# First two rows of a fused delta-rule and two-MoE kernel: an explicit numbered order, beta by row loads, paired norms, low halves on VectorE

## The chip, the cores and the metric

The kernel runs on one core of a Trainium2 chip. The metric is the device time of one execution in microseconds. A core has TensorE (PE; its weight loads are PEld), VectorE (DVE), ScalarE (ACT), GpSimd (POOL) and SyncE (SP, which issues most DMAs). Each engine works through its own queue in the order in which the program was written; semaphores hold an instruction until what it reads is there.

## The reference

Three layers follow each other: a delta-rule recurrence over 768 tokens for 4 x 8 heads of width 48, then two feed-forward layers on the 3072 tokens of width 384.

```python
k_n = k / (np.linalg.norm(k, axis=-1, keepdims=True) + 1e-06)
for t in range(S):                       # state: (B, H, D, D)
    kt, vt, bt = (k_n[:, :, t], v[:, :, t], beta[:, :, t, None])
    y[:, :, t] = np.einsum('bhd,bhde->bhe', q[:, :, t], state)
    v_old = np.einsum('bhde,bhd->bhe', state, kt)
    state = state + bt[:, :, :, None] * np.einsum('bhd,bhe->bhde', kt, vt - v_old)
...
xn = x / np.sqrt(np.mean(x * x, axis=-1, keepdims=True) + 1e-06) * rms_g
x = (silu(xn @ w_gate) * (xn @ w_val)) @ w_out
...
h = x @ w_in
out = (h * np.tanh(softplus(h))) @ w_out2
```

## The kernel before, in words

The recurrence is computed in 12 rows (chunks) of 64 tokens; two rows make a segment. A row needs the inverse of a triangular matrix made of beta and the Gram matrix of its normalised keys. The steps of a row are the stages of `chain_row` (L795): turn q (`q0`, `q1`), residual `r`, state product `y`, masked scores `p`, `v` (values, with ScalarE's copies at L863), state update `k` (L907, L912), outputs `o0`, `o1`, and the hand-over to the feed-forward layer `s`, `x`. Some stages work four rows ahead: norms `nA` (`norm`, L422), scaling `nB` (`scale_k`, L448), turning `c0`, `c1` (`turn_k`, L460) and the Gram product `g` (`products`, L471).

The inverse for segments 1 to 5 is made by `inlane` (L518), a long series of VectorE instructions (L514 to L610) that starts with one of ScalarE (L513) and is finished by `merge32` (L618) on TensorE and ScalarE. For segment 0 there is a quicker way for one row at a time: `quick_lane` (L647), some 29 VectorE instructions from L658 to L729, and then `quick_products` (L735), a chain of small products and copies between TensorE, VectorE (L750) and ScalarE (L758, L769, L630, L640). Row 2 needs what `inlane(1)` gives, row 4 what `inlane(2)` gives, and so on; `lanes` (L780) runs them side by side with the rows.

The feed-forward weights come as raw 64-bit floats and are converted to a high and a low fp32r half: `prepare_half` (L123) has ScalarE's Abs (L139), four VectorE operations on tile t (L144, L147, L152, L155), ScalarE's high copy (L166) and GpSimd's low subtraction (L169). `convs` (L173) runs twelve such halves for the pairs of part A, the part of the first layer that `gated` (L219) works on beside the rows. Part A's units are handed out per row by `DUE`: 0, 6, 5, then 11. After the last row what is left of part A and all of the rest are TensorE work with little waiting.

The order of the queues is written by Python generators. `merge` (L38) draws the next step from the stream that is least far in relation to its planned total; each row's loop merges the row with part A, conversion, `lanes` and some warm-up products (`warm`, L1019). The first row's start is a sequence of its own: norms one at a time, k0 scaled by VectorE and the others by GpSimd, T and G for rows 0 and 1, `quick_lane(0)` with 26 warm-up products, then a merge of `quick_products(0)` with the norms of k2 and k3 and `quick_lane(1)`; `inlane(1)` starts within row 0. beta reaches its layouts `bq` and `bl` by 32 small DMAs in `setup` (L357): eight issued by ScalarE and eight by SyncE (L363), sixteen by SyncE (L418).

Of the kernel before, what the change touches and what calls it, by code (L numbers as in the profile page):

```python
# [8 lines left out]
F32 = mybir.dt.float32  # L9
F32R = mybir.dt.float32r  # L10
# [10 lines left out]
    XB=2, WE=16, RB=4, TB=3, LANE=15.7, XL=1, HH=0, DPRE=5, WU0=24, WU1=35, WARM=[0, 0], CVS=[2.6, 9.0, 5.0, 13.1, 0], CVA=12, CVT=12.22, CVB0=0, CVB1=1.238, CVC=2.31, PSD=1, INV=1, Q=[0, 2.7, 1.2, 9.9, 0, 18.8, 2.8, 3.0, 11.5, 3.0, 11.0, 19.4], W=[22, 26], SQ=6, CVP=0, NE=2, BQ=3, NU=6, CVN=1, CVE=14.671, CVD=4.076, OFF=6.0,  # L21
    ROW="r nA q0 q1 S p T nB y X v Y k c0 o0 c1 o1 g".split(),
    R0="r q0 q1 p nA v k o0 o1 s0 nB s1 x0 c0 c1 g".split(),
    R2="r nA Y q0 q1 p nB y v k c0 o0 c1 o1 g".split(),
    R1="r nA q0 Y q1 y p nB v k o0 o1 s0 s1 x0 c0 c1 g".split(),
    DUE=[0, 6, 5, 11],
    PRE="t10 t11 c g1 c c w1 | t20 t21 g2 t30 t31 g3".split(),
    C=dict(n=0.2, q=0.5, r=1.4, y=1.1, p=1.2, v=1.2, o=0.9, k=1.2, s=0.1, x=0.45, c=0.4, d=0.4, g=1.2, h=1.2),
)

# [38 lines left out]
def kernel(  # L69
# [48 lines left out]
    count = [0]  # L118

    def prepare(get_pool, key, cut, act=True, **kw):  # L120
        return [prepare_half(half, get_pool, key, cut, act, kw) for half in range(2)]

    def prepare_half(half, get_pool, key, cut, act, kw):  # L123
# [19 lines left out]
        count[0] += 1  # L143
        (nc.gpsimd if count[0] <= P["CVP"] else nc.vector).tensor_scalar(  # L144
# [24 lines left out]
        nc.gpsimd.tensor_tensor(out=lo, in0=tv, in1=hi.bitcast(F32), op=ALU.subtract)  # L169
# [3 lines left out]
    def convs(pairs, wait=0):  # L173
# [5 lines left out]
        yield from delay(wait)  # L179
# [101 lines left out]
    def phase_b1():  # L281
# [33 lines left out]
        even, odd, top = (qc[:, 96 + i:97 + i] for i in range(3))  # L315
        NK = 5
# [9 lines left out]
        kT_t, A_t, X11_t, v_t, x_t, nr_t = {}, {}, {}, {}, {}, {}  # L326
# [30 lines left out]
        def setup():  # L357
            qsrc = beta[:, :, 0:2 * C].rearrange("b (j e) (r f h t) -> e f r (b j) h t", e=2, r=2, f=2, t=16)
            def load_bq(r, queue=nc.sync):
                for g in range(4):  # L360
                    for bp in range(2):
                        o = g * 32 + bp * 16
                        queue.dma_start(  # L363
                            out=bq[o:o + 16, r], in_=qsrc[(g // 2) ^ bp, g % 2, r, bp * 8:bp * 8 + 8]
                        )

            load_bq(0, nc.scalar)
            for r in range(4):
                load_k(r)
                nc.vector.memset(khp[r][:, :, D:64], 0.0)  # L370
                if r == 1:
                    load_q(0)
            load_bq(1)
# [16 lines left out]
            nc.vector.memset(X_[:, 0:272].rearrange("p (i x) -> p i x", x=17)[:, :, 0:1], 1.0)  # L390
            nc.vector.tensor_reduce(
# [20 lines left out]
            bsrc = beta.rearrange("b (j e) (s r f t) -> e f r (b j) s t", e=2, r=2, f=2, t=32)  # L412
            for e in range(2):
                for f in range(2):
                    for r in range(2):
                        for bp in range(2):
                            p0 = (e ^ bp) * 64 + f * 32 + r * 16 + bp * 8
                            nc.sync.dma_start(out=bl[p0:p0 + 8], in_=bsrc[e, f, r, bp * 8:bp * 8 + 8])  # L418
            load_k(4)
            nc.sync.dma_start(out=gT, in_=rms_g.rearrange("(k p) -> p k", p=128))  # L420

        def norm(r, sq=None):  # L422
# [6 lines left out]
            ss = ch.tile([128, 16], F32, tag="ss", name="ss", bufs=2)  # L429
            nc.vector.tensor_reduce(out=ss, in_=sq, axis=AX.X, op=ALU.add)  # L430
            nr = ch.tile([128, 16], F32, tag="nr", name="nr", bufs=2)
            if r < P["SQ"]:
                rt = ch.tile([128, 16], F32, tag="rn", name="rt", bufs=2)
# [14 lines left out]
        def scale_k(r, eng=nc.gpsimd):  # L448
            if r >= NR:
                return  # L450
            nr, kr = nr_t.pop(r), khp[r % NK][:, :, 0:D]
            rn = ch.tile([128, 16], F32, tag="rn", name="rn", bufs=2)
# [552 lines left out]
        for m in range(FA):  # L1005
            gens.append(prepare(lambda: wa, ("g", m), cols(w_gate, m)))
            gens.append(prepare(lambda: wa, ("v", m), cols(w_val, m)))
        for m in range(FA):
            gens.append(prepare(lambda: wa, ("o", m), rows(w_out1, m)))
        cv = convs(gens)  # L1010
# [17 lines left out]
        W_ = P["W"]  # L1028
        Q = P["Q"]
        sq = [xp.tile([128, KD, T], F32R, tag="xh", name="sq", bufs=XB) for _ in range(2)]  # L1030
        sq = [flat(t)[:, 0:16 * D].rearrange("p (u d) -> p u d", d=D) for t in sq]
        run(warm(W_[0]), norm(0), scale_k(0, nc.vector), norm(1, spare), scale_k(1))
        chain0 = chain_row(0)

        def ahead_of(names):
            for x in names:
                if x[0] == "t":
                    r, i = int(x[1]), int(x[2])
                    yield from turn_k(r, i, pre(i) if r else None)
                elif x[0] == "g":  # L1040
                    r = int(x[1])
                    yield from products(r)
                elif x[0] == "n":
                    yield from norm(int(x[1]), sq[int(x[1]) - 2])
                elif x[0] == "s":
                    yield from scale_k(int(x[1]))
                elif x[0] == "w":
                    yield from warm(W_[int(x[1])])
                elif x[0] == "c":
                    next(chain0)  # L1050
                    yield 1.0

        PRE = []
        for x in P["PRE"]:
            if x == "|" or not PRE:
                PRE.append([])
            if x != "|":
                PRE[-1].append(x)
        run(turn_k(0, 0), turn_k(0, 1), products(0))
        merge((quick_lane(0), 12), (ahead_of(PRE[0]), 6.0))  # L1060

        def reset():
# [4 lines left out]
        first = quick_products(0)  # L1067
        next(first)
        merge(
            (first, 5.0),  # L1070
            (seq(*[f(r, *a) for r in (2, 3) for f, a in ((norm, (sq[r - 2],)), (scale_k, ()))], quick_lane(1)), 12.5),
            (seq(delay(14.0), ahead_of(PRE[1])), 20.0),
            (budget(cv, Q[6]), Q[7]),
        )
        lane, laned, left = lanes(merges(1)), [0.0], []
        M1A = 4.0 * FA + KD
        ps_ds = [ps_d]
        part_a = gated((ps_u, ps_ds, hp, tp), range(FA), range(NR), get_xa, finish_a, next_x)
        for sg in range(NSEG):
            for rl in range(2):  # L1080
                r = 2 * sg + rl
                streams = [(chain_row(r) if r else chain0, cost(r))]
                due = P["DUE"][r] if r < len(P["DUE"]) else P["DUE"][-1]
                if due > 0:
                    off = P["OFF"] if r == 1 else 1.5 if r == 2 else 0
# [3 lines left out]
                if r < len(P["WARM"]):  # L1089
                    streams.append((warm(P["WARM"][r]), 0.22 * P["WARM"][r] + 0.1))  # L1090
                if r == 0:
                    lane1 = seq(reset(), inlane(1))
# [202 lines left out]
```

## Time and profile before

| | us |
|---|---|
| median of 3 runs | 1223.62 (1223.1 to 1226.09) |
| the profiled execution's own time | 1223.5 |
| its span, first to last instruction | 1221.8 |
| TensorE busy | 1125.6 (92%) |
| VectorE busy | 721.7 (59%) |
| ScalarE busy | 561.8 (46%) |
| GpSimd busy | 438.6 (36%) |

Times in the timeline count from the start of the span. The granted clock is the share of TensorE's full clock: 1.0 is 2.4 GHz, 0.5 is 1.2 GHz, and a stretch in between is a mean over both. A busy share over the whole span mixes stages with different limits, so the stages are looked at one by one. In a timeline row the last bracket gives idle time before the instruction and what ended it.

### The profile page before, as it was taken

The numbers are of one execution on the slowest core, as the hardware profiler recorded it, in microseconds if no ns is written. First come the engines' busy times: TensorE is split into PE (matmuls) and PEld (weight loads), VectorE is DVE, ScalarE is ACT, GpSimd is POOL, SyncE is SP. The second block draws the span as 40 slices with busy tenths as digits, with TensorE's granted clock in tenths as the row PEclk, the third lists the DMA queues.
The fourth block names the chain that finished last, engine by engine and source line by source line (L and its number), as shares of the span: only waits on it lengthen the run. The fifth ranks groups of instructions, "written<-read, shape, count | busy, mean of one in ns | idle before, by whom it ended". The sixth has DMA issues, their size and how long they took to land.

```text
span 1221.8 us, 32530 instructions
## 1 busy us (share of the span) xinstructions
PE 1125.6 (92%) x14176; PEld 1094.6 (90%) x14176; DVE 721.7 (59%) x1142; ACT 561.8 (46%) x1061; POOL 438.6 (36%) x392
## 2 busy tenths in 40 slices
PE   7675798999998779999999999988999999999998
PEld 6565688989898678999999999988999999999998
DVE  6789898887877658455555542367434433333333
ACT  2454656565655563211111110162757555555672
POOL 2123455353332444334434442234323332232232
PEclk8556699999998889999999999998999999999999
DMA  6224033333224443443333222421111101111101
GB/s 132 43 67 105 27 81 80 81 80 81 67 73 136 134 136 124 130 132 128 114 108 104 104 91 76 132 92 55 37 40 40 40 14 40 39 40 40 37 3 27
DMA packets 121695, 95.02 MB, mean 78 GB/s; under 512 B 81104, under 2 KB 104144, under 8 KB 121552
## 3 DMA queue, kind: packets, MB, share of 16 engines
q1 hardware_dynamic: 109264, 69.33, 20.7%
q10 hardware_dynamic: 12288, 23.61, 5.9%
q8 instruction: 111, 1.82, 0.6%
q14 instruction: 32, 0.26, 0.1%
HBM read 64.60 MB, written 28.31 MB: 76 GB/s over the span
## 4 chain that ended last, share of the span: by engine, by line
PE 62%; DVE 7%; ACT 3%; POOL 2%; issue 2%; DMA 1%; SPq 0%; DVEq 0%; POOLq 0%; ACTq 0%
PE pd L1191 5%; PE pd L1192 5%; PE pd L1190 5%; PE ph L216 5%; PE ph L215 5%; PE ph L217 5%; PE pd L232 3%; PE pd L233 3%; PE pd L234 3%; PE pg L215 3%; PE pv L215 3%; PE pg L217 3%; PE pg L216 3%; PE pv L217 3%; PE pv L216 3%
## 5 line engine op out<-in xcount | busy, mean ns | idle before, releaser
L1238 POOL TENSOR_TENSOR gl<-t,gh 128x512 fp32r<-128x512 f32 x96 | 125.2, 1304 | 253.2 <-DVE gh L1237 252.1
L215 PE MATMUL ph<-xh,wih 128*128 128x256 f32 x576 | 162.7, 282 | 5.4 <-DVE t L1234 5.4
L260 POOL TENSOR_TENSOR hl<-sg,hh 128x512 fp32r<-128x512 f32 x72 | 96.8, 1345 | 195.6 <-DVE hh L259 187.3
L216 PE MATMUL ph<-xl,wih 128*128 128x256 f32 x576 | 162.5, 282 | 0.0
L217 PE MATMUL ph<-xh,wil 128*128 128x256 f32 x576 | 162.5, 282 | 0.0
L232 PE MATMUL pd<-hh,woh 128*128 128x256 f32 x432 | 126.4, 293 | 14.4 <-ACT par L990 12.8
L1190 PE MATMUL pd<-wqh,gh 128*128 128x384 f32 x384 | 130.1, 339 | 2.2 <-DVE wqh L168 2.2
L1191 PE MATMUL pd<-wql,gh 128*128 128x384 f32 x384 | 130.4, 339 | 1.4 <-POOL wql L169 1.3
L1192 PE MATMUL pd<-wqh,gl 128*128 128x384 f32 x384 | 130.0, 339 | 0.0
L215 PE MATMUL pg<-xh,wgh 128*128 128x256 f32 x432 | 128.2, 297 | 0.0
L215 PE MATMUL pv<-xh,wvh 128*128 128x256 f32 x432 | 127.1, 294 | 0.0
L250 ACT ACTIVATE sg<-pg 128x512 f32<-128x512 f32 x72 | 43.2, 600 | 181.7 <-PE pg L217 164.2
L233 PE MATMUL pd<-hl,woh 128*128 128x256 f32 x432 | 124.3, 288 | 1.0 <-POOL hl L260 1.0
L216 PE MATMUL pg<-xl,wgh 128*128 128x256 f32 x432 | 123.7, 286 | 0.9 <-POOL xl L941 0.9
L234 PE MATMUL pd<-hh,wol 128*128 128x256 f32 x432 | 124.1, 287 | 0.0
L217 PE MATMUL pg<-xh,wgl 128*128 128x256 f32 x432 | 123.6, 286 | 0.0
L216 PE MATMUL pv<-xl,wvh 128*128 128x256 f32 x432 | 123.1, 285 | 0.0
L217 PE MATMUL pv<-xh,wvl 128*128 128x256 f32 x432 | 123.1, 285 | 0.0
L256 DVE TENSOR_TENSOR sg<-sg,pv 128x512 f32<-128x512 f32 x72 | 49.3, 685 | 113.9 <-PE pv L217 102.8
L215 PEld LDWEIGHTS ph<-xh,wih 128*128 128x128 f32 x576 | 109.7, 190 | 5.6 <-DVE t L1234 5.6
L1234 DVE TENSOR_TENSOR t<-t,ph 128x512 f32<-128x512 f32 x96 | 65.2, 680 | 82.3 <-ACT t L1232 82.3
L217 PEld LDWEIGHTS ph<-xh,wil 128*128 128x128 f32 x576 | 109.7, 190 | 0.0
(187 smaller groups left out, 2932.6 us busy)
## 6 DMA issues: line engine op xcount, KB each, us to landing
raw<-in_moe_w_out_dram SPq DMA_DIRECT2D x28, 384.0 KB
raw<-in_moe_w_in_dram SPq DMA_DIRECT2D x16, 384.0 KB
kh<-in_k_dram SPq DMA_DIRECT2D x24, 192.0 KB
qp<-in_q_dram SPq DMA_DIRECT2D x24, 192.0 KB
v<-in_v_dram SPq DMA_DIRECT2D x48, 96.0 KB
raw<-in_moe_w_gate_dram SPq DMA_DIRECT2D x12, 384.0 KB
raw<-in_moe_w_val_dram SPq DMA_DIRECT2D x12, 384.0 KB
xh_d<-xh SPq DMA_DIRECT2D x12, 384.0 KB
```

The source lines that it names most:

```text
L215: nc.tensor.matmul(ps[:, f, :], wh[:, kt, sl], xh[:, kt, :], start=(kt == 0), stop=False)
L216: nc.tensor.matmul(ps[:, f, :], wh[:, kt, sl], xl[:, kt, :], start=False, stop=False)
L217: nc.tensor.matmul(ps[:, f, :], wl[:, kt, sl], xh[:, kt, :], start=False, stop=(kt == KD - 1))
L232: nc.tensor.matmul(ps, wh[:, f, sl], hh[:, f, :], start=(i + f == 0), stop=False)
L233: nc.tensor.matmul(ps, wh[:, f, sl], hl[:, f, :], start=False, stop=False)
L234: nc.tensor.matmul(ps, wl[:, f, sl], hh[:, f, :], start=False, stop=last)
L260: nc.gpsimd.tensor_tensor(out=hl, in0=sg, in1=hh.bitcast(F32), op=ALU.subtract)
L1190: nc.tensor.matmul(ps, gh[:, f, sl], wh[:, f, :], start=(m + f == 0), stop=False)
L1191: nc.tensor.matmul(ps, gh[:, f, sl], wl[:, f, :], start=False, stop=False)
L1192: nc.tensor.matmul(ps, gl[:, f, sl], wh[:, f, :], start=False, stop=last)
L1234: nc.vector.tensor_tensor(out=t, in0=t, in1=ps, op=ALU.mult)
L1238: nc.gpsimd.tensor_tensor(out=gl, in0=t, in1=gh.bitcast(F32), op=ALU.subtract)
```

## The change

The first two rows no longer come from a start-up sequence and two merges. A function `plan` takes streams with explicit step numbers and always draws the one whose next number is lowest:

```diff
+def plan(*streams):
+    live = [[g, t, 0] for g, t in streams]
+    def at(x):
+        t = x[1]
+        return t[0] + t[1] * x[2] if isinstance(t, tuple) else t[min(x[2], len(t) - 1)]
+    while live:
+        x = min(live, key=at)
+        try:
+            w = next(x[0])
+        except StopIteration:
+            live.remove(x)
+            continue
+        x[2] += w if isinstance(x[1], tuple) else 1
...
+    R0="r q0 q1 p v k o0 o1 s0 s1 x0 x1 c0 c1 g".split(),
+    R1="r nA q0 q1 y p nB v k o0 o1 s0 s1 x0 c0 c1 g".split(),
+    CVS=[0, 0, 0, 0],
+    ROW0=[17.0, 17.5, 27.4, 36.4, 39.0, 39.5, 40.5, 42.0, 43.0, 44.0, 46.0, 52.0, 53.0, 54.0],
+    ROW1=[43.5, 46.5, 47.0, 47.5, 49.0, 50.0, 51.0, 65.0, 67.0, 68.0, 69.0, 71.0, 72.0, 73.0, 75.0, 76.0, 77.0],
+    QP0=[27.2, 28.0, 29.0, 30.0, 31.0, 32.0], QP1=[57.0, 58.0, 59.0, 60.0, 61.0, 62.0],
+    L0=(14.0, 1.0), L1=(41.5, 1.15), I1=(57.5, 1.3), CV=(57.0, 1.4), CVN0=99.0, FF=(56.0, 6.0),
+    CV0=[17.0, 18.0, 19.0, 31.1, 32.3, 33.5, 38.0, 38.1, 38.2],
+    K12=[7.3, 10.0, 11.9, 12.2], K34=[20.0, 29.6, 36.9, 37.5], S=[12.3, 28.1, 37.3, 37.6, 48.0],
+    T=[9.9, 36.6, 41.0, 43.0], G=[12.0, 39.0, 45.0, 48.0], END=97.0,
...
+        run(warm(24), norms([0], sq[2:]), scale_first(0))
+        plan(
+            (lanes_beta(False), [7.4]),
+            (norms([1, 2], [spare, sq[0]]), P["K12"]),
+            (norms([3, 4], sq[1:]), P["K34"]),
+            *[(seq(turned(r), products(r)), [P["T"][r], P["T"][r] + 0.2, P["G"][r]]) for r in range(4)],
+            *[(scale_first(r), [P["S"][r]]) for r in range(1, 5)],
+            (lanes_beta(True), [15.0]),
+            (quick_lane(0), P["L0"]),
+            (quick_products(0), P["QP0"]),
+            (quick_lane(1), P["L1"]),
+            (quick_products(1), P["QP1"]),
+            (seq(reset(), inlane(1)), P["I1"]),
+            (budget(cv, P["CVN0"]), P["CV0"] + [P["CV"][0] + P["CV"][1] * i for i in range(40)]),
+            (chains[0], P["ROW0"]),
+            (chains[1], P["ROW1"]),
+            (budget(part_a, P["DUE"][1]), P["FF"]),
+        )
```

In the lists, T and G are turning and Gram product of rows 0 to 3, S the scaling of k1 to k4, K12 and K34 the paired norms, L0 and L1 the quick inversions, QP0 and QP1 their products, I1 the in-lane inversion of segment 1 (a pair is a first number and a factor on the generator's own cost), CV0 and CV the conversion, FF part A. All twelve conversion halves are now drawn here; rows 2 and 3 have none. The 26 warm-up products go.

beta is loaded in four DMAs of eight whole rows each into `bnat`, and TensorE brings it into both layouts with selection matrices made once:

```diff
-            load_bq(0, nc.scalar)
...
-            load_bq(1)
...
+            load_k(0)
+            bsrc = beta.rearrange("b (j e) s -> e (b j) s", e=2)
+            for e in range(2):
+                for bp in range(2):
+                    p0 = (e ^ bp) * 16 + bp * 8
+                    nc.sync.dma_start(out=bnat[p0:p0 + 8], in_=bsrc[e, bp * 8:bp * 8 + 8])
+            load_k(1)
+            load_k(2)
+            load_q(0)
+            load_k(3)
...
+            nc.vector.memset(sel, 0.0)
...
+                    nc.vector.tensor_copy(to[:, f, z], pair)
...
+        def lanes_beta(wide):
...
+                    nc.tensor.matmul(ps, sel[:, int(wide), i], src_of, start=(i == 0), stop=(i == 3))
+            nc.scalar.copy(bl if wide else bq, ps)
+            yield 1.0
```

`norms(rs, scratch)` does the norms of two k tiles with one set of small operations (two Squares and two sums, then one root, five operations and a reciprocal on 32 columns); `scale_first` scales k0 to k4 on VectorE, where k1 to k4 were scaled by GpSimd. The low halves of these twelve conversions are subtracted by VectorE:

```diff
-        nc.gpsimd.tensor_tensor(out=lo, in0=tv, in1=hi.bitcast(F32), op=ALU.subtract)
+        low_by.tensor_tensor(out=lo, in0=tv, in1=hi.bitcast(F32), op=ALU.subtract)
...
-    def convs(pairs, wait=0):
+    def convs(pairs, at_once=0):
...
+        for g in gens[:at_once]:
+            next(g)
+            yield 0.2
+        for g in gens[:at_once]:
+            next(g)
+            next(g)
+            yield 1.4
+        for i, g in enumerate(gens[:at_once]):
+            for g in gens[i + depth:i + depth + 1]:
+                next(g)
+            for _ in gens[i]:
+                pass
+            yield 0.1
```

The loop over segments now begins at segment 1 and is otherwise as before, without warm-up products.

## Rows read from the trace of the kernel before

**Rows 1.** The page's slices: TensorE's busy tenths, 40 slices of 30.5 us each.

```profile
PE   7675798999998779999999999988999999999998
```

**Rows 2.** Stretches: us; busy us (count) of PE, PEld, DVE, ACT, POOL; clock; DMA.

```profile
47.80:70.50 22.70, 15.10 (x429) 13.38 (x433) 20.39 (x42) 13.11 (x24) 5.95 (x8) 0.50 0.22 55
70.50:139.00 68.50, 47.73 (x1052) 43.24 (x1046) 62.12 (x92) 34.12 (x82) 23.25 (x21) 0.62 0.28 71
143.40:201.80 58.40, 51.52 (x1301) 47.59 (x1299) 54.90 (x73) 34.74 (x80) 30.89 (x24) 0.94 0.35 81
201.80:262.50 60.70, 57.49 (x1360) 53.64 (x1360) 50.77 (x67) 37.36 (x90) 27.72 (x23) 0.97 0.30 77
```

**Rows 3.** VectorE's waits, 0 to 190 us: total us, times, longest us.

```profile
DVE v L826 <- PE pp L821: 6.2, 2, 4.6
DVE ss L430 <- ACT sq L428: 4.4, 1, 4.4
...
DVE h L406 <- ACT h L375: 4.4, 1, 4.4
```

**Rows 4.** Timeline (start us, us, engine, line): in-lane inversion of segment 1, next one.

```profile
70.58 1.28 DVE L514 SCALAR_TENSOR_TENSOR comp<-A,h,comp 128x1024 f32<-128x1024 f32 x1 [1.04 <-ACT comp L513]
...
137.01 1.98 DVE L610 STREAM_TRANSPOSE yc<-N__166 128x1024 f32<-128x1024 f32 x1
...
143.43 1.13 ACT L513 ACTIVATE comp<-A,h 128x1024 f32<-128x1024 f32 x1
```

**Rows 5.** Timeline: beta's DMA issues, first quick inversion, start of the second.

```profile
0.80 6.52 ACTq L363 DMA_DIRECT2D qc<-in_beta_dram  x8
...
12.91 6.17 SPq L363 DMA_DIRECT2D qc<-in_beta_dram  x8
...
20.34 0.39 DVE L651 TENSOR_SCALAR qc<-qc 128x32 f32<-128x32 f32 x2 [4.44 <-DMA qc<-in_beta_dram]
...
33.63 1.03 DVE L729 STREAM_TRANSPOSE YT<-e 128x512 f32<-128x512 f32 x1
...
47.84 0.40 DVE L658 TENSOR_SCALAR compq<-A,h 128x512 f32<-128x512 f32 x1
```

**Rows 6.** Timeline: prices of the quick products' chain, and the warm-up products.

```profile
15.33 1.99 PE L488 MATMUL pp<-kT 64*64 64x64 f32 x64
...
19.48 1.16 PE L488 MATMUL pp<-kT 64*64 64x64 f32 x64
...
22.95 6.07 PE L1021 MATMUL warm<-ident 128*128 128x128 f32 x52
...
38.74 1.18 ACT L758 COPY X11q<-pp 32x512 f32<-32x512 f32 x2 [16.47 <-PE pp L745]
...
53.01 1.92 PE L745 MATMUL pp<-YT,Zq 32*32 32x32 f32 x64
...
66.95 1.97 ACT L863 COPY ve<-pp 64x384 f32<-64x384 f32 x4
```

**Rows 7.** VectorE's groups, 70.5 to 139 us: busy us, mean ns, idle before.

```profile
L497 DVE TENSOR_TENSOR PT<-pp,mpos 128x512 f32<-128x512 f32 x2 | 1.3, 682 | 0.0
...
L826 DVE TENSOR_TENSOR v<-v,pp 128x384 f32<-128x384 f32 x2 | 1.0, 551 | 4.6 <-PE pp L821 4.6
...
L430 DVE TENSOR_REDUCE ss<-sq 128x16 f32<-128x768 f32 x1 | 0.9, 943 | 0.0
```

**Rows 8.** Timeline: scaling of k on VectorE; a low half on GpSimd.

```profile
12.41 0.96 DVE L454 TENSOR_TENSOR kh<-kh,rn 128x768 f32<-128x768 f32 x1
...
85.10 1.00 POOL L169 TENSOR_TENSOR wgl<-t,wgh 128x384 fp32r<-128x384 f32 x1 [3.26 <-ACT wgh L166]
```

**Rows 9.** Stretches, conversion's tile t alone: us; DVE, ACT, POOL; clock; DMA.

```profile
70.50:139.00 68.50, 18.03 (x30) 7.52 (x14) 11.49 (x7) 0.62 0.28 71
108.00:109.30 1.30, 1.10 (x2) 0.00 (x0) 0.00 (x0) 0.50 1.06 209
111.10:112.00 0.90, 0.71 (x2) 0.00 (x0) 0.00 (x0) 0.50 0.51 204
```

More of the change, by code (lines that the diff above doesn't have):

```diff
@@ L115, in seq, with prepare, prepare_half @@
             yield from g
[L118 to L123, printed above, removed]
+    def prepare(get_pool, key, cut, act=True, low=None, **kw):
+        return [prepare_half(half, get_pool, key, cut, act, low or nc.gpsimd, kw) for half in range(2)]
+    def prepare_half(half, get_pool, key, cut, act, low_by, kw):
         src, nk, nf = cut
@@ L178, in convs @@
         yield 0.1
-        yield from delay(wait)
+        for g in gens[:at_once]:
[11 more added lines that the diff above has]
+            yield 0.1
+        gens = gens[at_once:]
         next(gens[0])
@@ L324, in phase_b1 @@
         sx = kp.tile([128, B, 2, 2, D], F32, name="sx")
[L326 removed]
+        kT_t, A_t, X11_t, v_t, x_t, nr_t, rn_t = {}, {}, {}, {}, {}, {}, {}
         def part(i):
@@ L1027, in phase_b1 @@
         spare = rp.tile([128, 16, 64], F32, tag="PT", name="spare")[:, :, 0:D]
-        W_ = P["W"]
-        Q = P["Q"]
         sq = [xp.tile([128, KD, T], F32R, tag="xh", name="sq", bufs=XB) for _ in range(2)]
         sq = [flat(t)[:, 0:16 * D].rearrange("p (u d) -> p u d", d=D) for t in sq]
[L1032 to L1060, printed above, removed]
+        sq.append(ch.tile([128, 16, D], F32, tag="sq", name="sq"))
+        chains = [chain_row(0), chain_row(1)]
+        ps_ds = [ps_d]
+        part_a = gated((ps_u, ps_ds, hp, tp), range(FA), range(NR), get_xa, finish_a, next_x)
         def reset():
@@ L1065, in reset, with turned @@
             yield 1.0
[L1067 to L1073, printed above, removed]
+        def turned(r):
+            yield from turn_k(r, 0)
+            yield from turn_k(r, 1)
+        run(warm(24), norms([0], sq[2:]), scale_first(0))
[15 more added lines that the diff above has]
+            (budget(part_a, P["DUE"][1]), P["FF"]),
         )
         lane, laned, left = lanes(merges(1)), [0.0], []
[L1076 to L1079, printed above, removed]
+        for sg in range(1, NSEG):
             for rl in range(2):
                 r = 2 * sg + rl
-                streams = [(chain_row(r) if r else chain0, cost(r))]
+                streams = [(chain_row(r), cost(r))]
                 due = P["DUE"][r] if r < len(P["DUE"]) else P["DUE"][-1]
                 if due > 0:
-                    off = P["OFF"] if r == 1 else 1.5 if r == 2 else 0
+                    off = 1.5 if r == 2 else 0
                     streams.append((seq(delay(off), budget(part_a, due)), off + due))
```

97 lines of the change are left out of this document (56 added, 41 removed).

## The prediction

> **What bounds the kernel now.** I read the page's slices, then stretches of the first 262 us, then VectorE's waits there, then the timeline. TensorE's first five slices of 40 (to 153 us) stand at 5 to 7 tenths, of the other 35 all but two at 8 or 9 [rows 1]. That late part is fixed TensorE work; a change of the prologue can only move its beginning.
>
> The stretches show what sets that beginning [rows 2]. From 47.8 us to the end of the first full in-lane inversion at 139 us VectorE is busy 82.5 of 91.2 us and TensorE 62.8, at a granted clock of 0.50 and 0.62. So VectorE's queue is the bound there. Its large waits are few: 4.4 us each for ScalarE's h0, for a Square and for a DMA of beta, 6.2 in all for the residual's product [rows 3, 5]. The inversion ends with the transpose L610 at 138.99; the next segment's begins on ScalarE at 143.43 (L513) [rows 4]. From there segment pairs take 58.4, then 60.7 us, and in the latter TensorE is busy 57.5 [rows 2]: steady state, the same code in both kernels. My yardstick is therefore the first start of L514 (70.58), the second of L513 (143.43), and the length of the first pair. What they lose or win goes to the end one for one.
>
> **The change, stretch by stretch.** The profiled execution took 1223.5 us (span 1221.8), level with the median of 1223.62.
>
> *A, to the end of the first quick inversion.* Out go ScalarE's eight beta issues (6.52 us), SyncE's eight (6.17) and sixteen later ones; four of 0.77 come in. VectorE waited for those of SyncE before it could start at 20.34 [rows 5]. Its new set-up (a memset, eight small copies) lies in the 4.4 us wait for h0, which goes; if it outlasts that, it reaches into the wait for G0's copies. The Squares of k1 and k2 now stand ahead of kT0's copies on ScalarE, and both loads are behind the four beta issues (3.1 us). I take G0's copies done at 17.7, bounds 16.9 and 20. The inversion itself took 20.34 to 34.66; it ends near 32 instead.
>
> *B, to the start of the second quick inversion.* Here the order costs. Before, T1 and G1 were made early, and the second inversion began at 47.84 [rows 5]. Now they are numbered behind row 0's values (36.4 against 36.6 and 39.0), so the whole chain of quick products comes first. At half clock [rows 6], from 32.3 when the first product is done: scores 1.99, second product 1.92, two blocks of 1.92 (ScalarE's 1.18 beside them): 40.1; copies of Z and A 1.18 each: 42.4; product 1.92, copies 1.18, merge 1.92, copies 1.18: 48.6; values 1.92, their copies 1.97: 52.5; kT1's copies 1.18, G1 1.99, its copies 1.18: 56.9; a dozen hand-overs of about 0.1: 58. That is 10 us later than before. In those 26 us VectorE has only some 15 of ready work (three converted halves, sums, scales, a mask's product, an addition). The numbers make it worse: the root for k3 and k4 (36.9) stands on ScalarE behind the values' copies, and k3's scale and the lows stand behind it on VectorE. At full clock (1.16 for 1.99) eight blocks give back 0.83 each, 6.6 us.
>
> The 26 warm-up products, 6.07 us of TensorE at 22.95 [rows 6], go too. The stretch from 47.8 had 0.50 although they had run [rows 2], so I charge nothing; the bounds are 0 and those 6.6 us. *The Trainium skill, "TensorE: Matmul & The Clock Gate", Part 1, has the slow clock as the resting state, which activity lifts; by that, dropping them speaks against the change and the sum would be up to 6.6 us worse, had they kept the clock up; the row says that they did not.*
>
> *C, to the start of the in-lane inversion.* 14.3 us of quick inversion, and in its queue now: the residual's subtraction, 1.1 in two, with a wait like the present 4.6, as its product stands behind outputs and four turns of k2 and k3; k5's norm, about 2 (0.94 of it sums); k4's scale 0.96; masked scores 1.4; in all about 10 [rows 3, 7, 8]. So 58 + 24.3 = 82. TensorE has k4's turns, G4, a first unit of part A and the off product ahead of Zq: 5 us more, two and a half blocks that VectorE can't fill. Then Zq 0.7, product 1.92, X11's copies 1.18, ScalarE's 1.1 for the compare tile, hand-overs: L514 near 93 instead of 70.58, **+23**. Before, that step stood ahead of the second quick products; now it stands behind them.
>
> *D, the in-lane inversion.* VectorE's 62.1 us lose what moved into C (residual, Zq, scores, norm, one addition to the state: 6). They lose contention: 30 operations, seven and a half halves, took 18.03 us here, 2.40 a half, against 1.10 + 0.71 = 1.81 where GpSimd was off that tile [rows 9]: 8 x 0.59 = 4.7. They gain a ninth half, 1.8, and nine lows. No low on VectorE is shown; the one-input half of 0.71, 0.35, and GpSimd's own 1.00 bound it, and half of the 128x768 product's 0.96 is nearest in kind [rows 8, 9]: 0.5, together 4.5. 62.1 - 6 - 4.7 + 6.3 = 57.7. Waits: the first of these lows needs ScalarE's high copy, which is numbered behind row 1's values (65.4 against 65); by B's chain, some 17 us from Zq on, those copies end near 110, while VectorE comes to that low some 11 us after L514, at 104. With 6 us of wait D is 63.7 against 68.5: **-5**.
>
> *E, the first pair.* No conversion is left there: VectorE's 54.9 fall toward the 50.8 of the next pair [rows 2]: **-4** (bounds 0 and -4.1). The paired norms and the scales on VectorE (0.96 each, four) lie in B's waits, which cover them; without that cover the scales would cost 3.8, less what the pairing saves.
>
> Sum: +23 - 5 - 4 = **+14**: 1223.5 + 14 = 1237.
>
> **Rivals.** *Filled (faster).* Place: VectorE between its two quick inversions. If the ready work and the steps behind it fill the gaps, VectorE's own work sets the pace: 32, plus 15.7 in B and 20.4 in C without waits, puts L514 at 68; D is 57.7, E -4: -2.5 - 10.8 - 4 = -17, 1206. Most of it filled (L514 at 74, D 59): 3.5 - 9.5 - 4 = -10, **1213**. It decides if L514 starts before about 79. For it: the waits that go in A, and VectorE freed of GpSimd's traffic. Against: B's chain is TensorE's and ScalarE's, and VectorE's queue is in order.
>
> *Full clock (no change).* With B's and C's blocks at 1.16 L514 comes at about 81: +10 - 5 - 4 = +1, **1224.5**. For it: blocks closer together. Against: 0.50 where TensorE was busy 15.1 of 22.7 us [rows 2]. *The same section of the Trainium skill would grant the full clock to a TensorE kept busy; the trace agrees at 0.97 in the later pair.* To this case also belongs that the change does nothing since later pairs catch up; against, TensorE has 3 us of slack in one of them.
>
> *Slower still.* Lows at 1.00 (+4.5), A at 20 (+2.3), E at 0 (+4), one more wait in D: **1250**.
>
> **How the numbers follow.** The forecast with its slower neighbour 0.63, filled 0.25, no change 0.12. The range, 1212 to 1250, takes in most of the filled case and the upper bounds; the forecast's own is 1228 to 1250. About 0.3%, 3.7 us, can be told from no change: faster 0.25, same 0.12, slower 0.63.
>
> **What would show it.** Right: second L658 near 58, L514 near 93, D near 64, first pair near 54, VectorE waits of several us for the root of k3 and k4 and for a high copy. Wrong: a first L514 before 79, or a granted clock well over 0.50 from 35 to 90 us.

## The result and the profile after

The changed kernel took 1230.81 us (median of 4 runs, 1230.02 to 1231.63) beside 1223.97 for the kernel before: **+6.8 us, a ratio of 1.0053 (1.0036 to 1.0071)**. The direction was forecast; the size, +13.4 us (the sum's +14 before rounding), was not, though 1230.8 lies in the range. The profiled execution took 1230.23 us, its span is 1228.5, 6.7 more than before.

The page's slices of the kernel after, TensorE's busy tenths and its granted clock:

```profile
PE   6866099999998868999999999988999999999998
...
PEclk7668589999998989999999999998999999999999
```

The loss lies in the first five slices of 30.7 us, as with [rows 1]; in the fifth TensorE now works for less than a tenth. Behind them the two kernels look alike.

Timeline of the kernel after: the start of the second quick inversion, its last transpose, Zq, the start of the in-lane inversion, the first low half behind it, its last transpose, and ScalarE's start of the next one. They answer to [rows 4, 5].

```profile
54.47 0.48 DVE L741 TENSOR_SCALAR compq<-A,h 128x512 f32<-128x512 f32 x1
...
73.02 1.05 DVE L812 STREAM_TRANSPOSE YT<-e 128x512 f32<-128x512 f32 x1
...
78.62 0.69 DVE L833 TENSOR_TENSOR Zq<-pp,qc 128x512 f32<-128x512 f32 x1 [4.50 <-PE pp L828]
...
84.67 1.28 DVE L597 SCALAR_TENSOR_TENSOR comp<-A,h,comp 128x1024 f32<-128x1024 f32 x1 [4.70 <-ACT comp L596]
...
97.87 0.56 DVE L192 TENSOR_TENSOR wvl<-t,wvh 128x384 fp32r<-128x384 f32 x1 [5.16 <-ACT wvh L189]
...
145.59 1.92 DVE L693 STREAM_TRANSPOSE yc<-N__166 128x1024 f32<-128x1024 f32 x1
...
150.80 1.15 ACT L596 ACTIVATE comp<-A,h 128x1024 f32<-128x1024 f32 x1
```

The in-lane inversion starts at 84.67 instead of 70.58, **+14.1**. It takes 62.8 us to the end of its last transpose (147.51) instead of 68.4, -5.6, and the hand-over to ScalarE's next compare is 1.1 shorter. So the second compare starts at 150.80 instead of 143.43: **+7.4**. From there on, by the starts of that compare: first pair 57.2 instead of 58.4 (-1.2), second 63.0 instead of 60.7 (+2.3), third 60.8 instead of 61.0, and what is left of the span 1.6 shorter. 7.4 - 1.2 + 2.3 - 0.2 - 1.6 = 6.7.

Stretches of the kernel after (us; busy us (count) of PE, PEld, DVE, ACT, POOL; granted clock; DMA): from the end of the first quick inversion to the start of the second; to its last transpose; to the in-lane start; the in-lane inversion; the first and the second pair.

```profile
30.10:54.50 24.40, 19.38 (x641) 17.69 (x631) 15.37 (x33) 11.75 (x25) 0.00 (x0) 0.58 0.23 62
54.50:74.10 19.60, 14.63 (x424) 12.91 (x424) 18.39 (x40) 12.49 (x34) 6.68 (x10) 0.83 0.39 92
74.10:84.70 10.60, 8.62 (x339) 8.00 (x332) 1.37 (x5) 4.27 (x7) 2.55 (x3) 0.66 0.01 3
84.70:147.50 62.80, 26.68 (x580) 24.05 (x579) 56.44 (x91) 23.28 (x51) 5.33 (x6) 0.69 0.18 45
150.80:208.00 57.20, 50.83 (x1233) 47.00 (x1233) 50.18 (x67) 33.56 (x77) 27.11 (x21) 0.89 0.34 79
...
208.00:271.00 63.00, 59.32 (x1360) 55.25 (x1360) 50.71 (x67) 37.24 (x88) 27.62 (x22) 0.95 0.33 78
```

VectorE's column tells where the prologue loses: it has 9.0 us without work in the first stretch and 9.2 of the 10.6 us ahead of the in-lane start. Its waits up to 190 us, kernel after (total us, times, longest us):

```profile
DVE comp L597 <- ACT comp L596: 8.3, 2, 4.7
DVE nr L487 <- ACT rn L485: 7.4, 3, 6.8
DVE wvl L192 <- ACT wvh L189: 5.2, 1, 5.2
DVE Zq L833 <- PE pp L828: 5.0, 2, 4.5
```

The three large waits of [rows 3] are gone (a Square, h0, the residual); these came in their place. The root of k3 and k4 holds VectorE for 6.8 us, a high copy for 5.2, and Zq and the compare tile for 9.2 together, one behind the other.

### The profile page after: what moved, and what is told of

Same layout as the page of the kernel before. It is cut to its first block, busy times and chain, and to the rows that moved or that the text cites. A ratio compares the mean times of both kernels' runs of the same rounds, so it can differ in the third digit from the quotient of the medians.

```text
span 1228.5 us, 32421 instructions
## 1 busy us (share of the span) xinstructions
PE 1115.1 (91%) x14144; PEld 1084.4 (88%) x14144; DVE 722.0 (59%) x1155; ACT 560.4 (46%) x1061; POOL 416.2 (34%) x376
## 4 chain that ended last, share of the span: by engine, by line
PE 69%; DVE 18%; ACT 6%; issue 4%; POOL 2%; SPq 0%; DMA 0%; DVEq 0%; POOLq 0%; ACTq 0%
PE pd L1250 5%; PE pd L1251 5%; PE pd L1249 5%; PE ph L252 5%; PE ph L253 5%; PE ph L251 5%; DVE pr L628 4%; PE pd L268 4%; PE pg L251 4%; PE pd L269 3%; PE pd L270 3%; PE pg L252 3%; PE pg L253 3%; PE pv L251 3%; PE pv L253 3%
## 5 line engine op out<-in xcount | busy, mean ns | idle before, releaser
L296 POOL TENSOR_TENSOR hl<-sg,hh 128x512 fp32r<-128x512 f32 x72 | 98.0, 1361 | 195.4 <-DVE hh L295 174.8
L268 PE MATMUL pd<-hh,woh 128*128 128x256 f32 x432 | 126.6, 293 | 13.4 <-ACT par L1073 10.7
L1293 DVE TENSOR_TENSOR t<-t,ph 128x512 f32<-128x512 f32 x96 | 65.2, 680 | 82.0 <-ACT t L1291 82.0
L252 PEld LDWEIGHTS ph<-xl,wih 128*128 128x128 f32 x576 | 109.7, 190 | 0.0
```

The costliest lines, as they stand in the source:

```text
L252: nc.tensor.matmul(ps[:, f, :], wh[:, kt, sl], xl[:, kt, :], start=False, stop=False)
L268: nc.tensor.matmul(ps, wh[:, f, sl], hh[:, f, :], start=(i + f == 0), stop=False)
L296: nc.gpsimd.tensor_tensor(out=hl, in0=sg, in1=hh.bitcast(F32), op=ALU.subtract)
L1293: nc.vector.tensor_tensor(out=t, in0=t, in1=ps, op=ALU.mult)
```

## Experiments

Times of kernels are set against the kernel before run beside them, as ratios with a 95% interval; a stage's time comes from one profile of each kernel. "Second compare" is the start of ScalarE's L596 for segment 2, 143.4 before and 150.8 after.

### What holds the in-lane start

**T1 and G1 early.** My step B made the late start of the second quick inversion the cause. Two kernels bring the turn, scale and product of row 1 forward; the first moves the inversion's own number too:

```diff
-    L0=(14.0, 1.0), L1=(41.5, 1.15), I1=(57.5, 1.3),
+    L0=(14.0, 1.0), L1=(28.0, 1.15), I1=(57.5, 1.3),
-    S=[12.3, 28.1, 37.3, 37.6, 48.0], T=[9.9, 36.6, 41.0, 43.0], G=[12.0, 39.0, 45.0, 48.0],
+    S=[12.3, 12.3, 37.3, 37.6, 48.0], T=[9.9, 12.5, 41.0, 43.0], G=[12.0, 13.0, 45.0, 48.0],
```

> Turning and Gram product of row 1 and the scaling of k1 take the numbers 12.3 to 13.0 again, and the second quick inversion begins at 28.0 instead of 41.5, so that it lies in the gaps of the first chain. Order theory (the loss is the late start of the second quick inversion): the first L597 comes at 66 to 74 instead of 84.7, the in-lane inversion keeps its 63 us, and the time is 10 to 18 us below the changed kernel, at 1213 to 1221. Load theory (VectorE simply has more to do, with the lows, the scales and all conversions in the first two rows): the first L597 moves, but the inversion gets longer by as much, and the time stays within 3 us of 1231. Clock theory (TensorE's half clock after the dropped warm-up products stretches the chain): within 3 us of 1231, with the chain as long as before.

Measured: 1237.87 us, 1.0114 (1.0094 to 1.0134), slower still. Timeline of that kernel, start of the second quick inversion and of the in-lane one, and below it VectorE's waits from 30 to 150 us:

```profile
36.09 0.48 DVE L741 TENSOR_SCALAR compq<-A,h 128x512 f32<-128x512 f32 x1
...
86.45 1.28 DVE L597 SCALAR_TENSOR_TENSOR comp<-A,h,comp 128x1024 f32<-128x1024 f32 x1 [4.24 <-ACT comp L596]
```

```profile
DVE ss L513 <- ACT sq L511: 5.9, 1, 5.9
...
DVE Zq L833 <- PE pp L828: 4.4, 2, 3.9
DVE comp L597 <- ACT comp L596: 4.2, 1, 4.2
```

The quick inversion starts 18.4 us earlier and the in-lane stage 1.8 us later. B's event is real, but it is not what holds the in-lane start: row 0's tail was pushed back (its state's addition starts at 61.5 instead of 53.5) and row 1's head, Zq and the compare tile still stand behind it, each with its wait.

The second kernel left the inversion's numbers where they were.

> Only the turning and Gram product of row 1 and the scaling of k1 go early; the second quick inversion keeps its number 41.5. Order theory, as the prediction put it (the products stand behind the values): the inversion begins some 5 us earlier and the time falls by 4 to 6 us. If instead the number of the inversion in VectorE's own queue holds it (it stands behind the lows and the state addition, which wait for ScalarE), its start stays within 2 us of 54.5 and the time within 2 us of 1231. Load and clock theory: no change.

Measured: 1236.1 us, 1.0097 (1.0074 to 1.012). The inversion starts at 55.7, the in-lane stage at 85.6, the second compare at 152.5: making G1 early brings nothing while VectorE comes to its next step no sooner.

Both kernels are also 5 to 7 us slower than the changed one, which none of the theories had: their second compares come 1.7 to 2.3 us later, and their first pairs take 59.5 us instead of 57.2, with 17.8 us of half clock in them instead of 12.3.

**The in-lane stage ahead of quick products 1.**

```diff
-    I1=(57.5, 1.3)
+    I1=(52.0, 1.3)
```

> The in-lane inversion of segment 1 gets the number 52.0 and so stands ahead of the second quick products (57.0) on ScalarE and VectorE. Order theory: the 4.7 us wait ahead of the first L597 and part of the 4.5 ahead of Zq go, L597 comes at 76 to 80, and the time falls by 4 to 8 us, to 1223 to 1227. Load theory: the inversion is the same work, and with row 1's chain pushed back the time stays within 3 us of 1231.

Measured: 1226.55 us, 1.0023 (1.001 to 1.0036). Timeline of that kernel, in-lane start and last transpose:

```profile
75.53 2.24 DVE L597 SCALAR_TENSOR_TENSOR comp<-A,h,comp 128x1024 f32<-128x1024 f32 x1 [0.53 <-ACT comp L596]
...
138.87 1.91 DVE L693 STREAM_TRANSPOSE yc<-N__166 128x1024 f32<-128x1024 f32 x1
```

One number gives back 9.1 us at the start, 6.7 at the last transpose and 5.9 at the second compare (144.9). The wait for the compare tile shrinks from 4.7 to 0.5 us and the one for Zq is gone, as in-lane work now stands where VectorE had none. Within the stage the wait for a high copy grows from 5.2 to 8.6 us, so less of the gain is left at its end. So the in-lane start is held by **its place behind the second quick products**, as C says, not by the inversion's start, as B says.

**The root of k3 and k4 earlier.**

```diff
-    K34=[20.0, 29.6, 36.9, 37.5]
+    K34=[20.0, 29.6, 30.0, 30.3]
```

> The changed kernel with one number moved: the root of the norms of k3 and k4 is taken at 30 in place of 36.9, ahead of row 0's values, so that VectorE's wait of 6.8 us (42.8 to 49.6) ends earlier. Theory 'order' (every wait of VectorE ahead of the first in-lane inversion pushes its end): the wait shrinks by some 4 us, the second quick inversion starts 1 to 4 us earlier than 54.5, but the in-lane start stays behind the numbers of row 1's quick products: last in-lane transpose near 146 in place of 147.5, total 1229 to 1230.5. Rival 'the root's wait is on the path': all 4 us come out at the second compare (147) and total 1227.

Measured: 1232.38 us, 1.0061 (1.0042 to 1.0081), no gain in all. The wait shrinks from 6.8 to 4.5 us, the second compare comes at 147.2, 3.6 earlier as the rival had it; then the first pair takes 62.4 us instead of 57.2 and eats it. That pair's stretch in that kernel (same columns):

```profile
147.20:209.60 62.40, 56.67 (x1233) 52.47 (x1233) 50.17 (x67) 33.62 (x76) 26.81 (x21) 0.78 0.32 72
```

VectorE's work and the count of products are those of the changed kernel (50.18 us, 1233); TensorE needs 56.67 us for them instead of 50.83, at a granted clock of 0.78 instead of 0.89, and it idles no longer than there (5.7 us against 6.4). What is won ahead of the pair can be lost in it by the clock alone.

### The low halves

All twelve conversions' lows back on GpSimd:

```diff
-        low_by.tensor_tensor(out=lo, in0=tv, in1=hi.bitcast(F32), op=ALU.subtract)
+        nc.gpsimd.tensor_tensor(out=lo, in0=tv, in1=hi.bitcast(F32), op=ALU.subtract)
```

> All low halves go back to GpSimd. Load theory: VectorE is relieved of twelve times 0.55 us and the time falls by 4 to 6 us. My reckoning in the prediction (contention of 0.6 us a half comes back, and ScalarE's Abs waits for GpSimd): between no change and 3 us slower. Order theory says nothing of the lows but expects the first L597 to stay within 2 us of 84.7.

Measured: 1228.05 us, 1.004 (1.0022 to 1.0058); the interval overlaps that of the changed kernel. In the stage it shows: 60.4 us of in-lane inversion instead of 62.8, VectorE busy 54.98 instead of 56.44. Nine lows of 0.55 (4.9 us) left VectorE, but only 1.5 us of its work went, so its other operations took some 3.4 longer while GpSimd had the lows. The trace of this kernel, operations on tile t in the in-lane stage (minimum, median and maximum ns), and from its timeline the longer one of L170 with the low beside it:

```profile
L167 DVE TENSOR_SCALAR t<-t x8: 322/354/1446, 87.6 to 136.9; 128x384 f32<-128x384 f32 x8
L170 DVE TENSOR_SCALAR t<-t x8: 359/360/1040, 88.0 to 137.2; 128x384 int32<-128x384 int32 x8
```

```profile
103.03 0.99 POOL L192 TENSOR_TENSOR wgl<-t,wgh 128x384 fp32r<-128x384 f32 x1
103.20 1.04 DVE L170 TENSOR_SCALAR t<-t 128x384 int32<-128x384 int32 x1
```

An operation of 0.36 us takes 1.04 beside a low. The 1.45 of L167 stands beside another subtraction of GpSimd's (L296), which the changed kernel has as well. The Trainium skill, "GPSIMD Engine Reference", in the table of section 1, "Specifications", names GpSimd's SBUF interfaces as shared with VectorE; these rows agree.

Together with the in-lane stage at 52:

> Both single edits together: the low halves go back to GpSimd, and the in-lane stage of segment 1 starts at number 52 in place of 57.5. Theory 'two causes add up' (the lows on VectorE cost 2.8 us, the in-lane start behind row 1's values and quick products 4.3 us, and the two hold different stretches): 1230.8 - 2.8 - 4.3 = 1223.7, no different from the kernel before (1224.1); the second compare of ScalarE near 150.8 - 3.6 - 5.9 = 141 us. Rival 'one and the same wait' (both only bring the last in-lane transpose forward, and what is behind it then waits for row 1's head): no better than the in-lane edit alone, 1226 to 1227, second compare at 145.

Measured: 1228.63 us, 1.0032 (1.0008 to 1.0056); last transpose at 140.9, second compare at 145.0. The two edits do not add up. The in-lane stage at 52 alone ended its last transpose at 140.8 too: with the lows on GpSimd VectorE works 2.1 us less in that stage (53.33 against 55.42) and idles as much longer (11.8 us against 9.9).

### The granted clock

Before, TensorE had work in most of the in-lane stage. In the kernel after it idles at its end: waits of TensorE from 100 to 170 us, and two stretches.

```profile
PE pp L709 <- DVE X L689: 22.3, 1, 22.3
```

```profile
122.00:145.00 23.00, 0.68 (x8) 0.31 (x7) 22.62 (x34) 3.42 (x7) 0.00 (x0) 0.50 0.00 0
145.00:170.00 25.00, 16.60 (x495) 14.81 (x497) 17.38 (x29) 13.07 (x23) 7.91 (x5) 0.64 0.21 56
```

The clock is at 0.50 while TensorE waits, and stays low as the first pair begins.

**Filling that idle time** with 100 products whose results nobody reads:

```diff
+        def warm_gap(n):
+            late_ps = pre(0)
+            for _ in range(n):
+                nc.tensor.matmul(late_ps[:, 0, :], ident, ident)
+            yield 1.0
...
             (budget(part_a, P["DUE"][1]), P["FF"]),
+            (warm_gap(100), [200.0]),
```

> The changed kernel with 100 extra 128 x 128 matmuls behind the numbered steps, in the 22.3 us in which TensorE waits for the merges' operand (122.6 to 144.9 us). The second compare of ScalarE stays at 150.8 in either case. Theory 'clock' (the first pair of segments gave only 1.2 of the 4 us forecast because the granted clock stays at half until 163 us behind that idle time): the clock is full from some 130 us on, the products, gram and transposes of rows 2 and 3 up to 163 us take half their time, third compare at 205 to 206 in place of 208.0, total 1227 to 1229. Rival 'VectorE' (those rows wait for VectorE and ScalarE, so TensorE's clock is hidden): third compare at 208, total 1230.5 to 1231.5.

Measured: 1231.93 us, 1.0062 (1.0038 to 1.0086), no change; third compare at 210.8. The same two stretches in that kernel:

```profile
122.00:145.00 23.00, 21.39 (x244) 20.98 (x243) 22.62 (x34) 3.86 (x9) 0.00 (x0) 1.00 0.02 7
145.00:170.00 25.00, 15.94 (x406) 14.33 (x406) 17.75 (x29) 11.37 (x20) 7.90 (x5) 0.59 0.18 49
```

The filling did lift the clock, from 0.50 to 1.00. But then TensorE waits again (2.2, 1.9 and 5.7 us between 143 and 156), the half clock moves from 122.1 to 163.1 us to 148.5 to 169.0, and more of it lies in the first pair than before (17.5 us instead of 12.3): the pair takes 59.3. Neither theory had this; the clock's price was still open. The Trainium skill, "TensorE: Matmul & The Clock Gate", Part 1, has the slow clock as the state of rest; the first of these stretches agrees in both kernels.

**The 26 warm-up products given back**, whose loss I charged at nothing:

```diff
+            (warm(26), [18.5]),
             (lanes_beta(True), [15.0]),
```

> The changed kernel with the 26 matmuls of 128 x 128 given back that the change took out behind the first quick inversion's start (number 18.5). The forecast charged their loss at nothing. Theory 'nothing': quick inversion 1 from 16.05 to 30, first compare of ScalarE at 83.5, total 1230 to 1231.5; the matmuls are done before the first quick products. Rival 'clock': the stretch from 12.9 to 33.4 us, now at half clock, is at full clock from some 20 us on, row 0's products and copies come 1 to 2 us earlier, first compare near 82, total 1228.5 to 1229.5.

Measured: 1234.12 us, 1.0083 (1.0065 to 1.0102). The half clock begins at 27.5 us instead of 12.9, and the first compare comes at 82.1 instead of 83.5, as the rival had it; but the second comes at 151.9, 1.1 later than without these products, and the time is above what either theory had, for a reason that is not shown. The clock that was won early is worth nothing at the second compare, so nothing was the right charge.

**18 products at each pair's start**, where TensorE idles 2 us and the clock falls:

```diff
                 turn(qp, bp, QT, ("Q", r, bp))
+                if bp == 1 and r >= 4 and r % 2 == 0:
+                    fill = bank(4, 128)
+                    for _ in range(18):
+                        nc.tensor.matmul(fill[:, 0, :], ident, ident)
```

> The changed kernel with 18 matmuls of 128 x 128 behind the transposes of q in rows 4, 6, 8 and so on, where TensorE idles about 2 us once in each pair of rows and the granted clock falls to half behind it (210.9 to 217.7, 272.3 to 275.7, 333.7 to 337.2 us and further). Theory 'clock' (a pair takes 59.3 to 60.0 us with no half clock in it, 60.6 to 61.9 with 3.4 us, 62.2 to 63.1 with 6.8 us): with the idle time filled the half stretches go, pairs of 59.5 to 60, five pairs with 1.3 to 3 us each: total 1222 to 1226. Rival 'other' (pairs are long for another reason and the clock only shows it, or the matmuls delay more than they bring): pairs of 61 to 63, total 1230 to 1234.

Measured: 1235.61 us, 1.0096 (1.0073 to 1.0119), slower. Second and third pair of that kernel:

```profile
209.20:271.00 61.80, 60.81 (x1403) 57.19 (x1403) 50.80 (x67) 37.29 (x89) 27.69 (x23) 1.00 0.33 79
271.00:332.70 61.70, 60.23 (x1398) 56.61 (x1398) 50.79 (x67) 37.28 (x89) 27.67 (x22) 1.00 0.29 73
```

The half clock is gone from both, and the second pair is 1.2 us shorter, but the third 0.9 longer: TensorE is busy 60 of 62 us there, so the added products cost about what the clock gives. Of the 6.9 us by which the span is longer than the changed kernel's, 6.0 lie behind the fifth compare (902.7 us to the end instead of 896.7), where the later rows have such products too; why they cost that much there is not shown.

### Put together

**In-lane stage at 52, lows on GpSimd, root at 30, the 100 products**, and the same with the 18 products in each pair:

> Lows on GpSimd, in-lane at 52, the 100 matmuls in the idle time behind the numbered steps, and the root of the norms of k3 and k4 taken at number 30 in place of 36.9, which takes away VectorE's wait from 42.8 to 49.6 us. If the sum of the two causes (1223.7) and the clock (2 to 4 us) add up, and the wait for the root lies on the path that ends the first in-lane inversion (up to 4 of its 6.8 us): 1217 to 1222. If the root's wait only moves (the next thing that VectorE needs is the turned k of row 1 from ScalarE): 1220 to 1222. If the clock gives nothing either: 1223 to 1224.

Measured: 1224.98 us, 1.0 (0.9986 to 1.0015); second compare at 141.9. All of the loss is back, and no more.

> Lows on GpSimd, in-lane stage at 52, root at 30, the 100 matmuls (the kernel that came out level with the kernel before), and the 18 matmuls at each pair's start. If the clock theory holds: 1225 less 4 to 8, 1217 to 1221. If not: 1225 to 1228.

Measured: 1224.0 us, 1.0005 (0.9987 to 1.0023): the 18 products bring nothing here either; behind the fifth compare this kernel takes 902.9 us, the one without them 899.8.

**Everything early.** The same without the 18, with rows 1 to 3 turned and multiplied ahead and the in-lane stage at 46:

```diff
-    QP1=[57.0, 58.0, 59.0, 60.0, 61.0, 62.0],
-    L0=(14.0, 1.0), L1=(41.5, 1.15), I1=(57.5, 1.3),
-    K34=[20.0, 29.6, 36.9, 37.5], S=[12.3, 28.1, 37.3, 37.6, 48.0],
-    T=[9.9, 36.6, 41.0, 43.0], G=[12.0, 39.0, 45.0, 48.0],
+    QP1=[50.0, 51.0, 52.0, 53.0, 54.0, 55.0],
+    L0=(14.0, 1.0), L1=(28.0, 1.15), I1=(46.0, 1.3),
+    K34=[20.0, 29.6, 30.0, 30.3], S=[12.3, 12.3, 31.0, 31.3, 48.0],
+    T=[9.9, 12.5, 36.6, 36.9], G=[12.0, 13.0, 38.8, 39.0],
```

> Everything in one kernel: the turns and products of rows 1, 2 and 3 at numbers 12.5 to 39, the second quick inversion from 28 on, quick products 1 from 50, the in-lane stage from 46, the root of k3 and k4 at 30, lows on GpSimd, and the 100 matmuls in TensorE's idle time. Theory 'order' (the first in-lane inversion is held by what stands ahead of it in VectorE's queue, and its waits): first in-lane compare at 62 to 68, last in-lane transpose at 128 to 134, second compare at 134 to 140, total 1217 to 1223. Rival 'load' (VectorE is busy nearly all the time from 54 to 137 us, so what is put first only pushes row 0 and row 1 back): second compare at 142, as in the kernel with the in-lane stage at 52, total 1224 to 1227.

Measured: **1220.97 us, 0.9977 (0.9965 to 0.9989), faster than both kernels**: 3.2 us under the kernel before in medians. Timeline of that kernel (in-lane start, the 100 products, which the profile counts as 200, last transpose, row 2's residual, second compare by VectorE) and its stretches:

```profile
71.43 1.28 DVE L597 SCALAR_TENSOR_TENSOR comp<-A,h,comp 128x1024 f32<-128x1024 f32 x1 [0.43 <-ACT comp L596]
...
118.33 22.60 PE L1110 MATMUL pre<-ident 128*128 128x128 f32 x200 [1.62 <-DVE sg L292]
...
134.67 1.97 DVE L693 STREAM_TRANSPOSE yc<-N__166 128x1024 f32<-128x1024 f32 x1
...
142.07 1.02 DVE L909 TENSOR_TENSOR v<-v,pp 128x384 f32<-128x384 f32 x2 [1.81 <-PE pp L904]
143.01 1.55 DVE L597 SCALAR_TENSOR_TENSOR comp<-A,h,comp 128x1024 f32<-128x1024 f32 x1
```

```profile
122.00:145.00 23.00, 23.00 (x296) 22.66 (x295) 20.64 (x31) 10.95 (x20) 5.31 (x5) 1.00 0.07 24
145.00:170.00 25.00, 23.27 (x719) 21.05 (x712) 23.90 (x37) 12.92 (x29) 12.89 (x10) 1.00 0.37 78
...
141.20:196.60 55.40, 52.78 (x1376) 48.55 (x1368) 51.72 (x69) 33.57 (x77) 30.78 (x24) 1.00 0.36 82
```

The total is the one that "order" had forecast, but by stage the rival "load" was right: the last transpose ends at 136.6, the second compare comes at 141.2, hardly earlier than the 141.9 of the kernel above. What is new is a first pair of 55.4 us, without any half clock in it. Order and filling came together here, so two more kernels take them apart, and settle the lows too.

**Everything early without the 100 products:**

> The kernel with everything early, without the 100 extra matmuls; all numbers and the lows on GpSimd as there. Theory 'order' (the gain of that kernel comes from the order alone): second compare of ScalarE near 141, first pair 55 to 56, total 1220 to 1222. Rival 'clock' (the first pair was short because no half clock lay in it; without the filling the half stretch lies between some 125 and 165 us again): second compare near 141, first pair 57.5 to 60 with 12 to 20 us of half clock in it, total 1223 to 1226.

Measured: 1224.71 us, 1.0003 (0.9992 to 1.0014); second compare at 143.2. Its stretches:

```profile
122.00:145.00 23.00, 5.20 (x85) 4.25 (x83) 21.27 (x33) 9.45 (x14) 6.15 (x7) 0.60 0.06 18
145.00:170.00 25.00, 21.21 (x518) 19.32 (x520) 18.68 (x31) 11.74 (x28) 10.20 (x8) 0.68 0.39 82
...
143.20:202.70 59.50, 53.54 (x1237) 49.28 (x1235) 50.26 (x68) 33.62 (x77) 30.80 (x24) 0.85 0.33 76
```

17.7 us of half clock lie in the first pair and it takes 59.5 us: the clock rival, in each of its numbers but the second compare, which is 2 us late as well. The intervals of the two kernels do not meet, so the filling is worth some 0.26%, 3.2 us, here, where it brought nothing to the changed kernel. The 100 products end at 140.9 us, ahead of the pair, so the pair itself has no added work: with them it is 4.1 us shorter, for 17.7 us less of half clock.

**Everything early with the lows on VectorE:**

> The kernel with everything early and the 100 matmuls, but the low halves on VectorE as in the changed kernel. Theory 'the lows cost' (2.8 us when they alone were put back on GpSimd): second compare at 143 to 145, total 1223 to 1225. Rival 'only the wait cost' (the lows matter because the first of them waits for ScalarE ahead of in-lane operations; GpSimd's low slows VectorE's other operations as much as VectorE's own 0.55 us each costs): second compare 140.5 to 142.5, total 1220 to 1222.

Measured: 1224.45 us, 1.0009 (1.0 to 1.0019); second compare at 145.9. The theory that the lows cost holds, 0.32% or 3.9 us. Where, its timeline shows: the low halves of part A's output weights, then row 2's residual and the next compare on VectorE.

```profile
143.08 0.56 DVE L192 TENSOR_TENSOR wol<-t,woh 128x384 fp32r<-128x384 f32 x1 [2.58 <-ACT woh L189]
...
145.41 1.22 DVE L192 TENSOR_TENSOR wol<-t,woh 128x384 fp32r<-128x384 f32 x2
...
147.40 1.02 DVE L909 TENSOR_TENSOR v<-v,pp 128x384 f32<-128x384 f32 x2 [0.78 <-PE pp L904]
148.34 1.28 DVE L597 SCALAR_TENSOR_TENSOR comp<-A,h,comp 128x1024 f32<-128x1024 f32 x1
```

The in-lane stage itself ends 1.7 us later (138.3 against 136.6, 1.1 of it from its start), with VectorE's busy time in it the same within 0.3 us (55.9 of 65.8 us, 56.2 of 65.2). The rest, 3.6 us more from there to the residual (147.40 against 142.07 in all), is lows that stand ahead of the residual in VectorE's queue: four of them from 138.12 on, 2.3 us of work, and 2.58 us in which one waits for ScalarE's high copy; against these the residual's own wait is 1.0 us shorter. In these two kernels a low costs nothing that shows in the stage's busy time; it costs behind the stage, by its wait as much as by its own 0.55 us.

**The first pair against the clock.** Length of the first pair, by the starts of ScalarE's compare, and the half clock within it, by the granted clock of each trace:

| kernel | half clock in it, us | first pair, us |
|---|---|---|
| everything early | 0.0 | 55.4 |
| the same, lows on VectorE | 3.4 | 56.9 |
| before (conversion still in the pair) | 6.8 | 58.4 |
| in-lane stage at 52, lows, root, both fillings | 6.8 | 57.0 |
| after | 12.3 | 57.2 |
| lows on GpSimd | 16.6 | 58.9 |
| idle time filled | 17.5 | 59.3 |
| everything early, no filling | 17.7 | 59.5 |
| in-lane stage at 52 | 19.3 | 60.1 |
| root at 30 | 27.5 | 62.4 |

About a quarter of a us of pair for each us of half clock (7.0 over 27.5). Single kernels lie up to 1.4 us off that line, the six that the table leaves out included. That the clock sets the length, and does not only go with it, is shown by the two kernels that differ in the filling alone (4.1 over 17.7) and by TensorE's longer time for the same products with the root at 30. The second and third pairs of all kernels without the 18 products order themselves in the same way: 59.3 to 60.5 us with none (4 pairs), 60.6 to 61.9 with 3.4 us of half clock (11), 62.2 to 63.1 with 6.8 (13).

## Why the prediction was right in direction and wrong in size

**The yardstick held.** In-lane start, second compare and first pair give +6.2 of the span's +6.7. It missed that a later pair can differ at the same code: "the same code in both kernels", I wrote of steady state, and the second pair was 2.3 us longer, with 6.8 us of half clock in it instead of 3.4.

**A, first quick inversion.** It ends at 30.1 where I had 32: G0's copies were done in time for a start at 16.05, ahead of my lower bound of 16.9. Mis-sized by 1.9.

**B, start of the second quick inversion.** 54.5 against 58, of which A is 1.9. The chain took 24.4 us where I had 26, VectorE had 15.37 us of work in it where I had some 15, and the wait for the root came (6.8 us). The event was forecast well; that it sets what follows was wrong. With the inversion 18 us earlier the in-lane stage started no sooner. The bound of 6.6 us for the dropped warm-up products counted the half clock twice, as B's blocks were priced at half clock already.

**C is the step that failed, in size: +23 forecast, +14.1 measured.** Its own terms give 93, which is +22.4; the start came at 84.7. Of the 8.3 us, 3.5 are A and B, and 4.7 lie between the start of the inversion and its last transpose, 19.6 us instead of my 24.3. The term that was mis-sized there is the residual's wait, "a wait like the present 4.6": the residual's subtraction began at 58.24 without any idle time before it, and VectorE was busy 18.4 of the 19.6 us. I took a wait of the old order as a price of the new one; the outputs and four turns that I put ahead of its product did not make it late. The granted clock was 0.83 in that stretch, not the 0.50 that I priced the blocks at, which fits a residual's product that is there in time; a clock well over 0.50 from 35 to 90 us, where it was 0.67, was my own sign of an error. Zq and the compare tile came 10.6 us after the transpose, as forecast (11), each behind the wait that I named, and that is the part that one number gives back.

**D was right**: 62.8 us for a forecast of 63.7, the first low's wait 5.2 for 6, a low 0.55 for 0.5. The same stage with the lows on GpSimd shows both terms of the sum, 4.9 for the lows and some 3.4 of contention relieved (I had 4.5 and 4.7). I set them level; what decides is the lows behind the stage with the wait that they bring into VectorE's queue, and the run with everything early has them at 3.9 us in all.

**E: -4 forecast, -1.2 measured.** VectorE's load fell as forecast, from 54.9 to 50.2 us, but the pair did not follow it. TensorE idled 22.3 us ahead of it and came in at half clock: 12.3 us of it lie in the pair, 6.8 before. Without any half clock the pair takes 55.4, which is -3.0. At 6.8 us of half clock, as before, it takes 57.0 (the kernel with both fillings), which is -1.4; so the load that left seems worth less than half of the 4, with one pair of each kernel to go by, and the rest is the clock, which the idle time in D left behind and E had left out. I had priced D on VectorE alone and not asked what TensorE would do for the last third of it.

**The rivals.** "Filled" wanted a start before 79 us; the changed kernel has 84.7, and the kernels that put in-lane work into VectorE's waits have 71 to 76. Its mechanism is right, and its price was too high: everything filled was worth 3.2 us over the kernel before, with TensorE's idle time filled as well, where the rival had 10. "Full clock" had the in-lane start at 81 with the blocks at full clock; the clock was between its levels, and so was the start.

The forecast missed by two errors in opposite directions: C was 8 us too long, and E with the second pair 5 us too short. That the direction came out right owes to the second error: with E at -4 and an unchanged second pair the kernel would have lost under 2 us (6.7 - 2.8 - 2.3 = 1.6).

## What to carry to other kernels

In a queue that runs in order, ask of each step which wait stands ahead of it and what else could stand there; moving the producer earlier brings nothing while the consumer's place in its queue is the same. A wait of the old order is a price of the new one only if the trace can name what will be late. When an engine is given idle time, look at the stage behind it as well: here a quarter of the half-clock time that followed came out as length of the first pair.

## What the runs showed of the hardware

In these kernels half clock was moved more easily than removed: 100 products lifted a stretch of 23 us from 0.50 to 1.00 and the half clock came back in the next one, at 0.59, behind waits of 2 to 6 us; only where those waits were gone too (everything early, TensorE busy 23.27 of the next 25 us) did it stay at 1.00 to the end of the first pair. One kernel's runs go with the clock too: with the root at 30, ten runs took 1226.17 us at a mean granted clock of 0.941 up to 1237.85 at 0.928. And GpSimd's subtraction costs VectorE time without any dependency between them: operations of 0.35 us took up to 1.45 beside it.
